# Threshold attention and feed-forward in one kernel: fewer weight chunks in the first six slots, diagonals given later, another end for the last tile

## The chip, the cores and the metric

The kernel runs on one core of a Trainium2 chip. The metric is device time in microseconds (us) from the start of the program to its end. The kernel before takes 1440.85 us, the median of three runs (1439.65 to 1445.99). The execution that was profiled took 1440.71 us and its profile spans 1438.9 us. Below, PE is TensorE, ACT ScalarE, DVE VectorE, POOL GpSimd and SP SyncE.

## What is computed

For 8 batches and 8 heads of 576 tokens and 64 features, attention keeps only scores close to the row's maximum; the heads are then laid side by side (512 features), and a feed-forward block with a layer norm ahead of it is added to its own input:

```python
scores = scale * np.matmul(q, k.transpose(0, 1, 3, 2))
thresh = np.max(scores, axis=-1, keepdims=True) - tau
scores = np.where(scores >= thresh, scores, -1000000000.0)
scores = scores - np.max(scores, axis=-1, keepdims=True)
attn = np.exp(scores)
attn = attn / (np.sum(attn, axis=-1, keepdims=True) + 1e-09)
x = np.matmul(attn, v)                      # then (B, H, S, D) -> (B, S, H*D)
...
mu = np.mean(x, axis=-1, keepdims=True)
var = np.mean((x - mu) ** 2, axis=-1, keepdims=True)
xn = (x - mu) / np.sqrt(var + 1e-06) * g_ln
ch = np.maximum(xn @ w_ch1, 0.0) @ w_ch2    # 512 -> 2048 -> 512
out = x + ch
```

The weights come as 64-bit floats, so the kernel has to turn them into 32-bit floats itself.

## The kernel before

**Slots.** Each batch is done in `SLOTS` = 9 slots, 72 in all (the loop at L750). A slot takes 512 rows of scores: of one pair of heads, or, in the middle slot of a batch (`s == HP` = 4), what is left of all four pairs. A slot's attention work is: scores on PE (L384) into two PSUM areas; row maxima on DVE (L398) and thresholds on POOL (L402); exponentials on ACT (L409); mask and sum on DVE (L416) and a reciprocal (L420). Then the weights are turned and multiplied with the values (L538) in the next slot.

**Two ways of turning.** In batch 0 (slots 0 to 8) `turn_weights` multiplies them on PE with a diagonal matrix that holds the reciprocals (`tp` L100, `tr` L468). The four diagonals are made on ACT (L427), and the products are copied from PSUM by ACT (`em` L462, `rest` L477). From slot 9 on, `turn_blocks` scales on POOL (L429), transposes on DVE (`et`, L494), stores to DRAM (`scr`, L500) and loads back (L509, L510).

**Feed-forward.** The 4608 tokens form 16 groups of 288, two to a batch. When group g has all its attention output, PE makes its mean (L573), DVE subtracts it (`xc`, L579), and `ffn_steps` is put into a queue. It has 16 steps of the first product (`p1`, each ended by a relu on ACT, L649), the variance with its inverse root on DVE (`root`, L616), and four output tiles `p2` of 16 steps each. `add_to_x` multiplies an output tile on DVE (L596) and adds x on POOL (L597); `store` transposes it on DVE (L602); `send` stores it by four DMAs on SP (L609). `second_part` (L703) deals out these PE steps over the four quarters of each slot, at a rate set by `ready(g)` (L696): the quarter in which group g comes in. Group 0 is ready at quarter 24 (slot 6), group 1 at 42 (slot 10).

**Buffers.** PE's products outside the scores share the PSUM tag `ff`, which has two buffers: `tp`, `tr`, `p1`, `p2`, `mean`, `var`, and `pv` in the first slots.

**Weight conversion.** `Weights` cuts both matrices into 32 chunks of 128 by 512 numbers, 16 of each matrix. `fetch` loads a chunk by a DMA on SP (L243), `begin` starts it with two operations on DVE (L263, L267) and two on ACT (L271, L275), `carry` adds on POOL (L281), `mask` is one DVE operation (L290), and `end` scales chunks of the first matrix on ACT (L303). One `tick` does the next such part of up to four chunks, in the order end, mask, carry, begin. A slot has up to six ticks; the first six slots use `ticks` (L752): two in slots 0 to 2 and three in slots 3 to 5. So 15 chunks are begun when slot 6 starts. Raw and half-made chunks lie in borrowed memory (`w2`, `hidden`, `et`, `x`, and `stage`); a number beside each piece says up to which chunk it may be used (L210 to L216). A feed-forward step is held back until its chunks are given.

**Order.** Every engine carries out its instructions in the order in which this code gives them; nothing is reordered by a planner. `aside`, `stores` and `at_quarter` are lists of calls that are given later, at fixed points of the loop.

Of the kernel before, what the change touches and what calls it, by code (L numbers as in the profile page):

```python
# [8 lines left out]
F32 = mybir.dt.float32  # L9
# [3 lines left out]
ALU = mybir.AluOpType  # L13
# [5 lines left out]
def kernel(  # L19
# [31 lines left out]
    nc = tc.nc  # L51
# [4 lines left out]
    HP = H // 2  # L56
    NK = DM // 128
# [3 lines left out]
    TOK = S // 2  # L61
    QH = 256
    SLOTS = 2 * HP + 1
    NG = 2 * B
# [9 lines left out]
    ffn = ctx.enter_context(tc.tile_pool(name="ffn", bufs=2))  # L74
# [8 lines left out]
    ident = consts.tile([128, 128], F32, name="ident")  # L83
# [6 lines left out]
    hidden = consts.tile([128, ND, TOK], F32, name="hidden")  # L90
# [33 lines left out]
    def load_v(u):  # L124
# [13 lines left out]
        out=tau_sb, in_=bass.AP(tensor=tau.tensor, offset=tau.offset, ap=[[0, 128], [1, 1]])  # L138
# [5 lines left out]
    for t in rests + v_rest:  # L144
# [9 lines left out]
        out=scl_sb, in0=tau_sb, scalar1=0.0, scalar2=SCALE, op0=ALU.is_ge, op1=ALU.mult  # L154
# [11 lines left out]
    class Weights:  # L166
# [13 lines left out]
        def __init__(self):  # L180
            self.chunks = [
                (w1_sb[i][:, c : c + WC], w_ch1[i * 128 : (i + 1) * 128, c : c + WC], i)
                for c in range(0, DF, WC)
                for i in range(NK)
            ] + [
                (
                    w2_sb[:, m, d : d + 4].rearrange("p d c -> p (d c)"),
                    w_ch2[d * 128 : (d + 4) * 128, m * 128 : (m + 1) * 128].rearrange(
                        "(d p) c -> p d c", p=128
                    ),  # L190
                    None,
                )
                for m in range(NK)
                for d in range(0, ND, 4)
            ]
            self.n1 = NK * (DF // WC)
            self.fetched = self.begun = self.carried = self.masked = self.ended = 0
            self.raw, self.made, self.due, self.ticks = {}, {}, [], 2
            flat = lambda t: t.rearrange("p a b -> p (a b)")

            x_room = ffn.tile([128, NK, TOK], F32, tag="x", bufs=3, name="x_room")
            stage = consts.tile([128, 8, WC], F32, name="stage")
            et = att.tile([128, NB, 128], F32, tag="et", bufs=1, name="et0")

            n1 = self.n1
            self.free = []
            for t, n, before in (  # L210
                (w2_sb.rearrange("p m d c -> p (m d) c"), ND // 2, lambda p: n1 + 2 * p),
                (hidden, 4, lambda p: 10),
                (et, 2, lambda p: 2 * n1),
                (x_room, 1, lambda p: 2 * n1),
                (stage, 4, lambda p: 2 * n1),
            ):  # L216
                for p in range(n):
                    self.free.append((before(p), -1, flat(t)[:, p * 2 * WC : (p + 1) * 2 * WC]))
# [87 lines left out]
        def tick(self):  # L306
            self.ticks += 1
            if self.ended < self.masked:
                self.end()
            if self.masked < self.carried and self.due[self.masked] <= self.ticks:  # L310
                self.mask()
            if self.carried < self.begun:
                self.carry()
            if self.begun < self.fetched:
                self.begin()
# [95 lines left out]
    def weights(es, thr, divide):  # L411


        den = small.tile([128, 4], F32, tag="den", name="den")
        for i in range(4):
            nc.vector.scalar_tensor_tensor(  # L416
                out=es[:, i], in0=blocks[i], scalar=thr[:, i : i + 1], in1=es[:, i],
                op0=ALU.is_ge, op1=ALU.mult, accum_out=den[:, i : i + 1],
            )
        nc.vector.reciprocal(den, den)  # L420
        diags = []
        for i in range(4):
            if not divide:
                if i % 2 == 0:
                    two = ffn.tile([128, TOK], F32, tag="o", bufs=6, name="diag")
                diags.append(two[:, i % 2 * 128 : i % 2 * 128 + 128])
                nc.scalar.mul(diags[i], ident, den[:, i : i + 1])  # L427
                continue
            nc.gpsimd.tensor_scalar(  # L429
                out=es[:, i], in0=es[:, i], scalar1=den[:, i : i + 1], scalar2=1.0,  # L430
                op0=ALU.mult, op1=ALU.mult,
            )
        return diags


# [77 lines left out]
    groups, sums = {}, {}  # L513
# [74 lines left out]
    def run_all(calls):  # L588
        now = calls[:]
        calls.clear()  # L590
        for fn in now:
            fn()

    def add_to_x(g, m, p2, rb):
        o = ffn.tile([128, TOK], F32, tag="o", bufs=6, name="o")
        nc.vector.tensor_mul(o, p2, rb)  # L596
        nc.gpsimd.tensor_tensor(out=o, in0=o, in1=groups[g][:, m], op=ALU.add)  # L597
        aside.append(lambda: store(g, m, o))

    def store(g, m, o):  # L600
# [4 lines left out]
    def send(g, m, ot):  # L605
        b, t = divmod(g, 2)
        for i in range(4):
            f = m * 128 + 32 * i
            nc.sync.dma_start(  # L609
                out=out[b, t * TOK : (t + 1) * TOK, f : f + 32].rearrange(  # L610
                    "(n r) c -> r n c", r=32
                ),
                in_=ot[32 * i : 32 * i + 32].rearrange("p (n c) -> p n c", c=32),
            )
# [81 lines left out]
    def ready(g):  # L696

        if g < 2:
            return (24, 42)[g]
        b, t = divmod(g, 2)  # L700
        return QUARTERS * (b * SLOTS + (HP, 2 * HP)[t] + 2) + (2, 4)[t]

    def second_part(n, i):  # L703

        nonlocal issued, owed
        if not queue:
            return
        at = QUARTERS * n + i
        g = issued // STEPS
        left = sum(ROOM[t % QUARTERS] for t in range(at, ready(g + 1))) if g + 1 < NG else 0  # L710
        owed += ((g + 1) * STEPS - issued) * ROOM[i] / left if left > 0 else 8


        got = 1 if i in (0, QUARTERS - 1) else 2
        while queue and (owed >= 0.5 or got == 1 and i in (0, QUARTERS - 1)):
            got = next(queue[0], None)
            if got is None:
                queue.pop(0)
                got = 1
            elif got == 0:  # L720
                owed = 0.0
                break
            else:
                issued += 1
                owed -= 1
# [7 lines left out]
    conversion = Weights()  # L733
# [15 lines left out]
    load_v(1)  # L749
    for n in range(NS):  # L750
        b, s = divmod(n, SLOTS)
        ticks = (1, 3, 4)[: 2 + n // 3] if n < 6 else range(1, 7)  # L752

        def tick(i):
            if i in ticks:
                conversion.tick()

        scores(b, s)
        run(n, -1)
        rest = exponentials()  # L760
        es, thr = next(rest)
        run(n, 0)
        conversion.fetch(2)
        run_all(stores)
        second_part(n, 0)
        next(rest, None)

        u = (n + 1) // SLOTS * HP + (n + 1) % SLOTS
        if (n + 1) % SLOTS < HP and u < len(units):
            turn(u)  # L770
            if u + 1 < len(units):
                load_qk(u + 1)
        run_all(aside)
        tick(1)
        run(n, 1)
        second_part(n, 1)
        tick(2)
        blocks_go = by_blocks(b * HP)
        diags = weights(es, thr, blocks_go)
        run_all(aside)  # L780
        run_all(stores)
        tick(3)
        run(n, 2)
        second_part(n, 2)
        tick(4)
        box = []
        if blocks_go:
            scr = turn_blocks(s, es)
            at_quarter(n + 1, 0, lambda s=s, scr=scr, box=box: box.append(fetch(s, scr)))
        else:  # L790
            made = turn_weights(s, es, diags)
            at_quarter(n + 1, -1, next, made)
            at_quarter(
                n + 1, 0 if s <= HP else -1, lambda made=made, box=box: box.append(next(made))
            )
        at_quarter(
            n + 1, 1 if b == 0 and s <= HP else 3,
            lambda b=b, s=s, box=box: values_of(b, s, box[0]),
        )
        if s in (HP, 2 * HP):  # L800
            group_ready(2 * b + (s > HP))
        run_all(aside)
        conversion.fetch(2)
        tick(5)
        run(n, 3)
        if b == 0 and s < HP - 2:
            load_v(s + 2)
        elif n >= SLOTS - 2 and (n + 2) % SLOTS < HP and n < NS - 2:
            load_v((n + 2) // SLOTS * HP + (n + 2) % SLOTS)
        second_part(n, 3)  # L810
        tick(6)
        run_all(aside)
# [37 lines left out]
```

## Time and profile before

| stretch, us | length | PE busy | DVE busy | ACT busy | what it is |
|---|---|---|---|---|---|
| 14.00 to 50.63 | 36.63 | 26.90 | 32.03 | 25.46 | slots 0 to 2 |
| 50.63 to 93.11 | 42.48 | 31.24 | 42.07 | 35.92 | slots 3 to 5 |
| 93.11 to 182.00 | 88.89 | 81.22 | 74.39 | 56.27 | slots 6 to 8, half of 9 |
| 182.00 to 1432.70 | 1250.70 | 1246.51 | 718.76 | 302.98 | the rest, to the last product |
| 1432.70 to 1438.90 | 6.20 | 0.00 | 0.94 | 0.00 | the end |

A stretch in which an engine is busy for nearly its whole length is set by that engine. A slot begins on DVE with two L398: at 50.63, 65.17, 79.68, 93.11, 123.20, 149.08, 168.44 and 194.94 for slots 3 to 10. In a timeline a line gives start, duration, engine, line of the kernel, operation, what is written from what, and count; in brackets how long the engine had been idle and what ended that. SPq is the queue of DMAs that SP gives.

### The profile page before, as it was taken

What the parts mean: (1) busy time and instruction counts of PE and PEld (TensorE: products, weight loads), DVE (VectorE), ACT (ScalarE), POOL (GpSimd) and SP (SyncE); (2) the same over time, 40 slices, a digit from 0 to 9 for tenths busy, and PEclk for the clock granted to TensorE, in tenths of its full rate; (3) what the DMA queues carried; (4) which work ended last, traced back from release to release, by engine and by line L of the source; (5) the groups of instructions that cost most, each with busy time, mean ns of one, the idle gap of its engine ahead of it and who ended that gap; (6) DMA issues with size and microseconds to landing.
All of it is one profiled execution on the core that took longest, in us unless ns stands there. A gap on an engine that the chain in (4) does not pass through costs nothing.

```text
span 1438.9 us, 29660 instructions
## 1 busy us (share of the span) xinstructions
PE 1389.7 (97%) x12168; PEld 852.3 (59%) x12168; DVE 870.5 (60%) x1492; ACT 421.9 (29%) x818; POOL 439.5 (31%) x681
## 2 busy tenths in 40 slices
PE   4879999999999999999999999999999999999998
PEld 3655665655556555655556555665556555565664
DVE  5998857556665666556665565656665666656111
ACT  3886513132222313132221312213132222213020
POOL 2344342333323233232322233232332323222100
PEclk8999999999999999999999999999999999999999
DMA  9622456558855587557855577556775578455301
GB/s 226 173 70 82 90 130 164 163 136 172 178 145 144 142 182 169 143 134 170 188 152 145 147 151 175 142 145 146 173 177 146 131 170 185 135 145 136 79 6 17
DMA packets 466840, 205.12 MB, mean 143 GB/s; under 512 B 275024, under 2 KB 428368, under 8 KB 466704
## 3 DMA queue, kind: packets, MB, share of 16 engines
q1 hardware_dynamic: 461936, 202.64, 57.9%
q8 instruction: 95, 1.56, 0.5%
q10 hardware_dynamic: 4736, 0.59, 0.4%
q14 instruction: 41, 0.34, 0.1%
q0 software_dynamic: 32, 0.00, 0.0%
HBM read 119.41 MB, written 83.76 MB: 141 GB/s over the span
## 4 chain that ended last, share of the span: by engine, by line
PE 89%; DVE 4%; ACT 2%; SPq 1%; issue 1%; DMA 1%; POOL 0%; POOLq 0%; ACTq 0%; DVEq 0%
PE p L100 67%; PE sc L538 10%; PE sc L384 10%; PE tp L100 1%; DVE e L416 1%; DMA em<-scr 1%; DVE neg L398 1%; SPq L500 1%; PE mean L100 0%; PE var L100 0%; DVE w L263 0%; ACT e L409 0%; PE tr L468 0%; SPq L129 0%; SPq L133 0%
## 5 line engine op out<-in xcount | busy, mean ns | idle before, releaser
L100 PE MATMUL p<-xc,w 128*64 128x288 f32 x4096 | 517.5, 408 | 6.5 <-ACT hidden L649 4.5
L100 PE MATMUL p<-hidden,w 128*64 128x288 f32 x4096 | 513.6, 407 | 0.0
L100 PEld LDWEIGHTS p<-xc,w 128*64 128x64 f32 x4096 | 291.8, 137 | 216.3 <-ACT hidden L649 14.4
L100 PEld LDWEIGHTS p<-hidden,w 128*64 128x64 f32 x4096 | 295.3, 137 | 199.1 <-issue 9.3
L398 DVE TENSOR_REDUCE neg<-sc 128x2 f32<-128x1152 f32 x144 | 188.8, 1352 | 250.1 <-PE sc L384 250.1
L409 ACT ACTIVATE e<-sc,neg 128x576 f32<-128x576 f32 x288 | 194.4, 742 | 261.7 <-DVE neg L398 256.2
L429 POOL TENSOR_SCALAR e<-e,den 128x576 f32<-128x576 f32 x252 | 188.5, 766 | 240.5 <-DVE den L420 240.4
L416 DVE SCALAR_TENSOR_TENSOR e<-sc,thr,e 128x576 f32<-128x576 f32 x288 | 219.1, 811 | 27.8 <-ACT e L409 27.8
L494 DVE STREAM_TRANSPOSE et<-e 128x1152 f32<-128x1152 f32 x112 | 153.6, 1375 | 78.3 <-POOL e L429 58.2
L649 ACT ACTIVATE hidden<-p 128x288 f32<-128x288 f32 x256 | 105.7, 413 | 284.5 <-PE p L100 282.9
L384 PE MATMUL sc<-kT,qT 64*128 64x384 f32 (+3 forms) x1024 | 150.2, 424 | 20.0 <-DVE qT L344 10.1
L402 POOL TENSOR_SCALAR thr<-neg,low_sb 128x2 f32<-128x2 f32 x144 | 41.9, 291 | 352.2 <-DVE neg L398 343.3
L384 PEld LDWEIGHTS sc<-kT,qT 64*128 64x128 f32 x1024 | 94.2, 191 | 77.2 <-issue 27.5
L538 PE MATMUL sc<-em,v_in 128*64 128x256 f32 (+1 forms) x1408 | 131.4, 330 | 2.1 <-DMA em<-scr 2.1
L555 ACT COPY x<-sc 128x256 f32<-128x256 f32 x60 | 22.3, 372 | 316.9 <-PE sc L538 291.9
L538 PEld LDWEIGHTS sc<-em,v_in 128*64 128x64 f32 x1408 | 86.2, 138 | 41.6 <-issue 2.9
L597 POOL TENSOR_TENSOR o<-o,x 128x288 f32<-128x288 f32 x64 | 51.4, 804 | 151.4 <-DVE o L596 151.4
L596 DVE TENSOR_TENSOR o<-p,rb 128x288 f32<-128x288 f32 x64 | 28.1, 439 | 103.5 <-PE p L100 103.0
L564 POOL TENSOR_TENSOR sum<-sum,x 128x256 f32<-128x256 f32 (+1 forms) x64 | 32.7, 511 | 71.8 <-ACT x L555 69.3
L655 POOL TENSOR_TENSOR sq<-sq 128x288 f32<-128x288 f32 x48 | 38.8, 808 | 42.1 <-ACT sq L653 39.6
L564 POOL TENSOR_TENSOR sum<-x 128x256 f32<-128x256 f32 (+1 forms) x32 | 16.7, 523 | 98.8 <-ACT x L555 57.3
L538 PE MATMUL sc<-rest,v_rest 128*64 128x256 f32 (+1 forms) x352 | 44.4, 329 | 0.0
(130 smaller groups left out, 715.0 us busy)
## 6 DMA issues: line engine op xcount, KB each, us to landing
scr<-et SPq DMA_DIRECT2D x252, 288.0 KB, 4.8
em<-scr SPq DMA_DIRECT2D x63, 1024.0 KB, 5.9
out_dram<-ot SPq DMA_DIRECT2D x256, 36.0 KB, 4.2
q_in<-in_q_dram SPq DMA_DIRECT2D x124, 72.0 KB, 3.4
k_in<-in_k_dram SPq DMA_DIRECT2D x120, 72.0 KB, 2.6
v_in<-in_v_dram SPq DMA_DIRECT2D x64, 128.0 KB, 4.5
rest<-scr SPq DMA_DIRECT2D x63, 128.0 KB, 5.9
w<-in_moe_w_ch_dram SPq DMA_DIRECT2D x10, 512.0 KB, 5.9
```

Source lines behind the costliest of these rows:

```text
L100: nc.tensor.matmul(out[r], lhsT=lhsT[:, r], rhs=rhs, **flags)
L384: nc.tensor.matmul(sc[h][64 * i : 64 * i + 64 if s == HP else 128, at : at + n], lhsT=ql[r] if s == HP else qT[r, half, j * 128 : (j + 1) ...
L398: nc.vector.tensor_reduce(out=neg[:, i], in_=pairs[h], axis=AXL.X, op=ALU.max, negate=True,)
L402: nc.gpsimd.tensor_scalar(out=thr[:, i], in0=neg[:, i], scalar1=-1.0, scalar2=low_sb, op0=ALU.mult, op1=ALU.add,)
L409: nc.scalar.activation(es[:, i], blocks[i], func=AF.Exp, bias=neg[:, i : i + 1])
L416: nc.vector.scalar_tensor_tensor(out=es[:, i], in0=blocks[i], scalar=thr[:, i : i + 1], in1=es[:, i], op0=ALU.is_ge, op1=ALU.mult, accum_o ...
L429: nc.gpsimd.tensor_scalar(out=es[:, i], in0=es[:, i], scalar1=den[:, i : i + 1], scalar2=1.0, op0=ALU.mult, op1=ALU.mult,)
L494: nc.vector.transpose(et[:, :, 64 * h : 64 * h + 64].rearrange("p n (j c) -> p j n c", j=2), es[:, 2 * h : 2 * h + 2].rearrange("p j (n c) ...
L538: nc.tensor.matmul(dst[64 * h : 64 * h + 64], lhsT=vt[:, c, h, :] if c < J else vr[:, h, :], rhs=pick(em[:, c] if c < J else er, hp, h), s ...
L564: nc.gpsimd.tensor_tensor(out=sums[g][:, cols], in0=x[:, 0, cols] if c == 1 else sums[g][:, cols], in1=x[:, c, cols], op=ALU.add,)
L597: nc.gpsimd.tensor_tensor(out=o, in0=o, in1=groups[g][:, m], op=ALU.add)
L649: nc.scalar.activation(hidden[:, d], p1, func=AF.Relu)
```

## The change

Five edits go together.

1. `ticks` is `(1, 3)` in all of the first six slots. So 12 chunks instead of 15 are begun when slot 6 starts, and the rest follow from slot 6 on. The borrowed pieces of `hidden` may be used only up to chunk 7 (before: 9), because the feed-forward writes `hidden` from slot 6 on; those of `et` only up to chunk 27 (before: 31). In slots 5 to 8 there is one more `fetch`.
2. The diagonals are taken out of `weights` into `diagonals`. In slots 0 to 4 and 8 they are given where they were; in slots 5 to 7 only after the third tick and the feed-forward steps of quarter 2. The aim is that relus on ACT don't stand behind diagonals that wait for DVE.
3. Group 1 is ready at quarter 43 instead of 42.
4. The last output tile of all (`g == NG - 1`, `m == NK - 1`) is added to x on DVE instead of POOL.
5. Its four stores are given by two queues, SP and ACT in turn, instead of SP alone.

```diff
-                (hidden, 4, lambda p: 10),
-                (et, 2, lambda p: 2 * n1),
+                (hidden, 4, lambda p: 8),
+                (et, 2, lambda p: 28),
...
-        diags = []
-        for i in range(4):
-            if not divide:
-                if i % 2 == 0:
-                    two = ffn.tile([128, TOK], F32, tag="o", bufs=6, name="diag")
-                diags.append(two[:, i % 2 * 128 : i % 2 * 128 + 128])
-                nc.scalar.mul(diags[i], ident, den[:, i : i + 1])
-                continue
+        for i in range(4 if divide else 0):
...
+        return den
+
+    def diagonals(den):
+
+        diags = []
+        for i in range(4):
+            if i % 2 == 0:
+                two = ffn.tile([128, TOK], F32, tag="o", bufs=6, name="diag")
+            diags.append(two[:, i % 2 * 128 : i % 2 * 128 + 128])
+            nc.scalar.mul(diags[i], ident, den[:, i : i + 1])
         return diags
...
-        nc.gpsimd.tensor_tensor(out=o, in0=o, in1=groups[g][:, m], op=ALU.add)
+        last = (g, m) == (NG - 1, NK - 1)
+        engine = nc.vector if last else nc.gpsimd
+        engine.tensor_tensor(out=o, in0=o, in1=groups[g][:, m], op=ALU.add)
...
-            nc.sync.dma_start(
+            last = (g, m) == (NG - 1, NK - 1)
+            (nc.scalar if last and i % 2 else nc.sync).dma_start(
...
-            return (24, 42)[g]
+            return (24, 43)[g]
...
-        ticks = (1, 3, 4)[: 2 + n // 3] if n < 6 else range(1, 7)
+        ticks = (1, 3) if n < 6 else range(1, 7)
...
-        diags = weights(es, thr, blocks_go)
+        den = weights(es, thr, blocks_go)
+        if n <= HP or n == 2 * HP:
+            diags = diagonals(den)
         run_all(aside)
         run_all(stores)
+        if HP < n < SLOTS:
+            conversion.fetch(2)
         tick(3)
         run(n, 2)
         second_part(n, 2)
+        if HP < n < 2 * HP:
+            diags = diagonals(den)
         tick(4)
```

## The prediction

> **What bounds the kernel now.** First the page's busy shares and 40 slices, then five stretches of the span by engine.
>
> ```profile
> PE 1389.7 (97%) x12168; PEld 852.3 (59%) x12168; DVE 870.5 (60%) x1492; ACT 421.9 (29%) x818; POOL 439.5 (31%) x681
> ...
> 50.63:93.11 42.48, 31.24 (x404) 23.99 (x400) 42.07 (x66) 35.92 (x72) 20.10 (x23) 1.00 0.35 106
> 93.11:182.00 88.89, 81.22 (x773) 54.65 (x775) 74.39 (x118) 56.27 (x108) 36.48 (x36) 0.98 0.32 82
> 182.00:1432.70 1250.70, 1246.51 (x10731) 751.04 (x10727) 718.76 (x1241) 302.98 (x589) 366.76 (x594) 1.00 0.60 145
> 1432.70:1438.90 6.20, 0.00 (x0) 0.00 (x0) 0.94 (x2) 0.00 (x0) 0.79 (x1) 0.83 0.15 24
> ```
>
> Columns: stretch, length, busy time of PE, PEld, DVE, ACT, POOL, clock, DMA share, GB/s. From 182 us to the last matmul PE idles 4 of 1251 us, so its work there is fixed and the time is that work plus the idle time ahead of and behind it. Only two places can give anything: the first 182 us and the last 6.2. Slots 3 to 5 (50.63 to 93.11, between the pairs of row maxima, L398) are VectorE's: busy 42.07 of 42.48 us. Its timeline at the end of slot 3:
>
> ```profile
> 59.00 0.18 DVE L420 RECIPROCAL den<-den 128x4 f32<-128x4 f32 x1
> 59.10 1.22 DVE L290 SCALAR_TENSOR_TENSOR hidden<-hidden 128x512 f32<-128x512 f32 x1
> 60.24 1.52 DVE L263 TENSOR_SCALAR w<-w 128x512 uint32<-128x512 uint32 x1
> 61.80 0.69 DVE L267 SCALAR_TENSOR_TENSOR w<-w 128x512 uint32<-128x512 uint32 x1
> 62.41 0.69 DVE L290 SCALAR_TENSOR_TENSOR hidden<-hidden 128x512 f32<-128x512 f32 x1
> 63.01 1.52 DVE L263 TENSOR_SCALAR w<-w 128x512 uint32<-128x512 uint32 x1
> 64.56 0.69 DVE L267 SCALAR_TENSOR_TENSOR w<-w 128x512 uint32<-128x512 uint32 x1
> 65.17 2.61 DVE L398 TENSOR_REDUCE neg<-sc 128x2 f32<-128x1152 f32 x2
> ```
>
> Two ticks of weight conversion (mask L290, begin L263 and L267) stand between the reciprocal and the next maxima. In slots 6 to 9 PE's gaps end with ScalarE:
>
> ```profile
> 93.61 2.87 PE L100 MATMUL tp<-diag,e 128*64 128x128 f32 x48 [1.81 <-ACT em L462]
> 106.16 2.16 PE L100 MATMUL p<-xc,w 128*64 128x288 f32 x16 [1.00 <-ACT hidden L649]
> 111.08 3.81 PE L100 MATMUL p<-xc,w 128*64 128x288 f32 x20 [2.76 <-ACT hidden L649]
> 170.05 1.09 PE L100 MATMUL tp<-diag,e 128*64 128x128 f32 x16 [0.69 <-ACT em L462]
> ```
>
> **What the Trainium skill says.** "SBUF — State Buffer", Who interferes with whom: a VectorE instruction with two SBUF inputs, or a tensor_scalar in two-port mode, blocks against GpSimd, for the whole instruction. The trace agrees: L263 takes 0.42 us at 53.76 but 1.52 at 63.01, beside GpSimd's carry (L281, 62.66 to 64.24). "PSUM — Partial Sum Buffer", Engine vs sequencer instructions: ScalarE's, VectorE's and GpSimd's queues are strict FIFO. It agrees: the relu at 110.63 comes behind two ticks and four diagonals although its product was ready. "Perfetto Trace Analysis", Optimization Strategy: a repeating gap on the saturated engine can mean too few buffers for the next tile. The gap before the second, third and fourth `tp` of slot 9 (0.69, 0.68, 0.68 us) is that: an open `p2` leaves one of two `ff` buffers. "DMA: Bandwidth & Descriptors", Issuing engines are not separate DMA queues: a second issuing engine saves only issue time.
>
> **The change part by part.**
>
> Third tick out of slots 3 to 5. In slots 3 and 4 it is 62.41 to 65.17 and 76.92 to 79.68: 2.76 us each. PE's scores of the next slot end at 61.2, before 62.41, so VectorE stays the limit. ScalarE then has per slot exponentials 2.6, copies 2.1 + 0.5 + 0.3, diagonals 1.2 and two ticks of 1.75 (its three lines L303, L271, L275 together): 10.2 us, in a slot that falls from 14.5 to 11.8. Gain 5.5 us. In slot 5 PE sets the next step: scores end 90.22, mean 90.76. There ScalarE's fourth-tick work disappears and the diagonals go behind the third tick's three ops; they end about 90.9, so the copies of `em` no longer hold PE 1.81 us. First product of the feed-forward about 1.9 us earlier. Together 7.4.
>
> Diagonals later in slots 6 and 7. In slot 6 the relus go ahead of the diagonals. With exponentials ending 1.9 us earlier I place the relu of step 2 at 103.85 in the old count, so the next product waits 0.8 instead of 1.0; then two ticks (3.5 us) still stand ahead of the relu of step 3, so 1.85 instead of 2.76. Gain 1.1. In slot 7 the first tick now carries a scaling (L303, 0.61) ahead of a relu: loss 0.6.
>
> Twelve chunks instead of 15 are begun when slot 6 starts. Slots 6 and 7 begin six each as before; the surplus lands in slot 8 (five begun instead of four) and slot 9 (three instead of one). In slot 8 PE's step is 21.5 us against VectorE's 12.2 up to the sums L416, so PE doesn't wait there.
>
> Group 1 ready one quarter later, with late chunks 30 and 31. This is where I expect the gain to go. In the order in which the changed code gives instructions, `mean` of group 1 comes in slot 10 after 16 matmuls of the third output tile and 12 of the fourth. Both tiles hold an `ff` buffer, so `mean` waits for VectorE to read the third (L596), which is queued behind slot 10's maxima, transposes, a mask and four L416. In the kernel before, that tile ended in slot 9 and was read at 191.78, ahead of `mean` at 197.24. Ahead of those maxima VectorE also has the begins of chunks 30 and 31, whose loads find no free piece before the second fetch of slot 9 and so are queued on SyncE behind the four `scr` stores, which wait for the transposes of `et`. Behind those begins on VectorE stand all of slot 10's sums, and PE waits for them through that one buffer. Lines for the prices:
>
> ```profile
> 184.27 2.84 DVE L494 STREAM_TRANSPOSE et<-e 128x1152 f32<-128x1152 f32 x2 [0.57 <-POOL e L429]
> 187.13 3.80 SPq L500 DMA_DIRECT2D scr<-et  x4
> 159.59 0.44 SPq L243 DMA_DIRECT2D et<-in_moe_w_ch_dram  x1
> 165.52 0.69 ACT L271 ACTIVATE et<-et 128x512 int32<-128x512 uint32 x1 [0.20 <-DMA et<-in_moe_w_ch_dram]
> ```
>
> Count from S, the start of slot 9's scores on PE (166.13 before). L416 ended S+15.3 before, set by ScalarE's copies; VectorE comes later now, 15.5 taken. To the end of the transposes 5.5 (181.5 to 187.0): S+21. `scr` issue 3.9, two loads and landing 5.9 (159.59 to 165.5): S+31. Begin and carry block 1.6, `ot` 0.5, maxima 2.6, transposes with their wait 2.2, mask 0.7, L416 and reciprocal 3.1, L596 0.4: about S+42. PE needs scores 2.1, `tp`, `tr` and gaps 8.0, 52 matmuls at 0.243 = 12.6, values 2.2: slot 10 begins S+24.9, then 2.1 + 28 x 0.243: it wants `mean` at S+33.9. New wait about 8.2 us. Bounds: if the loads land ahead of VectorE's need, only L416's queue counts, some 2.3; if VectorE enters slot 9 5 us late and the loads take longer, 11. I take 8.2. A single 0.7 us wait of PE at 204.2 (on L596) falls away.
>
> Tail. The last tile: multiply 1432.73, GpSimd 1433.34 to 1434.13, transpose 1434.16; an add on VectorE (0.45, as L596) starts the transpose at about 1433.7: 0.45. Four stores took SyncE 1.81 us to issue; two each on two queues save 0.9. ScalarE is idle there. Gain 1.35.
>
> Pieces of `hidden` only to chunk 7 and `et` only to chunk 27, and the extra fetch in slots 5 to 8: loads change places, none is added; in slots 0 to 5 they land ahead of use as before. Zero.
>
> Sum: 7.4 + 1.1 - 0.6 - 8.2 + 0.7 + 1.35 = 1.75; 1440.85 - 1.75 = 1439.1.
>
> **Rivals.** (a) The wait in slot 10 is short, 2.3 us: for it speaks that loads of 512 KB landed in 4.7 us too, and that the tick order may fall better; against it, FIFO order. Gain 7.65: 1433.2, and near 1432 if slot 6 loses its gaps altogether. (b) No gain early: ScalarE takes VectorE's place in slots 3 to 5 (35.92 of 42.48 us busy already), saving only 3 us instead of 7.4, with the same wait in slot 10. Sum -2.65: 1443.5, slower. Against it: the two-tick slot 1 took 11.7 us with 2.2 of transposes besides. (c) VectorE, still loaded in slots 7 and 8 (25.9 us of work in slot 7, all busy), is so late that slot 9's scores wait too and the slot 10 wait reaches 11: another 3 to 6 us, 1442 to 1445.
>
> **How the numbers follow.** Forecast 0.60, (a) 0.24, (b) 0.06, (c) 0.10. Predicted time 1439.1. The range takes in the forecast with both ends of the slot 10 wait (1433.2 to 1442) and the near half of (c): 1432.5 to 1443. Half a per cent is 7.2 us: under 1433.6 only most of (a), 0.20; over 1448 only the far edge of (c), 0.03; between them 0.77.
>
> **What would show it.** Right: maxima of slots 3, 4 and 5 about 11.8 us apart; first feed-forward product near 89.8; a PE gap of some 8 us before `mean` L100 in slot 10, released by L596's successor; VectorE idle in slot 9 for a weight load; last store issued 1.35 us sooner after the last matmul. Wrong: that gap under 3 us (then 1433), slots 3 to 5 still over 13 us, or new PE gaps before L384 in slots 7 to 9.

## The result and the profile after

The changed kernel takes 1450.35 us (median of 6 runs, 1449.02 to 1456.76), the kernel before in the same session 1440.96 us: ratio 1.0067, 95% interval 1.0045 to 1.009. It is 9.4 us slower. The forecast was 1439.1, at most 1443. The profiled span grew from 1438.9 to 1448.2 us.

PE first: the timeline of the changed kernel, its pieces with a gap ahead of them, and the first product of the feed-forward. (Its line numbers run up to 6 higher than before: L416 and earlier are unchanged, the copy of the values is L558, the relu L655, the multiply of an output tile L599, the `scr` stores L503.)

```profile
87.29 2.87 PE L100 MATMUL tp<-diag,e 128*64 128x128 f32 x48 [0.74 <-ACT em L465]
...
90.86 7.97 PE L100 MATMUL p<-xc,w 128*64 128x288 f32 x64
...
99.83 2.16 PE L100 MATMUL p<-xc,w 128*64 128x288 f32 x16 [1.00 <-ACT hidden L655]
103.58 1.68 PE L100 MATMUL p<-xc,w 128*64 128x288 f32 x12 [1.59 <-ACT hidden L655]
122.34 6.53 PE L100 MATMUL p<-xc,w 128*64 128x288 f32 x52 [1.35 <-ACT hidden L655]
156.74 3.73 PE L384 MATMUL sc<-kT,qT 64*128 64x384 f32 x16 [2.52 <-ACT x L558]
...
193.26 4.21 PE L384 MATMUL sc<-kT,qT 64*128 64x384 f32 x16 [9.77 <-ACT x L558]
206.75 0.71 PE L100 MATMUL mean<-sum,avg_sb 128*64 128x288 f32 x4 [1.95 <-DVE o L599]
```

Down to 104 us it goes much as forecast: the `em` wait is 0.74 instead of 1.81, the first product starts at 90.86 instead of 97.18, the gap of 2.76 is 1.59. Then three new waits stand where the kernel before had none: the scores of slot 9 (2.52), the scores of slot 10 (9.77) and `mean` (1.95). The first two end with ScalarE's copy of the values. In the stretches (columns as before: length, then busy PE, PEld, DVE, ACT, POOL, clock, DMA share, GB/s) the gain and the loss stand side by side:

```profile
50.00:85.00 35.00, 25.52 (x325) 20.01 (x322) 34.69 (x46) 28.76 (x56) 15.35 (x16) 1.00 0.39 115
85.00:200.00 115.00, 105.58 (x1018) 72.98 (x1016) 92.29 (x151) 67.08 (x130) 48.63 (x52) 0.99 0.34 89
...
50.00:85.00 35.00, 30.37 (x402) 23.82 (x400) 34.39 (x52) 31.20 (x62) 14.67 (x19) 1.00 0.29 84
85.00:200.00 115.00, 95.14 (x875) 66.04 (x876) 89.13 (x135) 63.23 (x123) 46.42 (x46) 0.94 0.39 102
```

The first two lines are the kernel before, the other two the changed one. PE is busy 4.85 us more in the first stretch and 10.4 us less between 85 and 200, at a lower clock. The cause is read across the engines, from the timeline around 190 us:

```profile
181.33 4.20 SPq L503 DMA_DIRECT2D scr<-et  x4
...
181.85 0.68 PE L541 MATMUL sc<-rest,v_rest 128*64 128x256 f32 x4
...
182.28 1.21 PE L100 MATMUL p<-hidden,w 128*64 128x288 f32 x8
185.63 2.86 SPq L243 DMA_DIRECT2D stage<-in_moe_w_ch_dram  x2
...
191.70 0.68 ACT L271 ACTIVATE stage<-stage 128x512 int32<-128x512 uint32 x1 [18.66 <-DMA stage<-in_moe_w_ch_dram]
191.70 0.43 DVE L263 TENSOR_SCALAR x_room<-stage 128x512 uint32<-128x512 uint32 x1 [10.05 <-DMA stage<-in_moe_w_ch_dram]
...
192.27 0.68 ACT L275 ACTIVATE x_room<-stage 128x512 f32<-128x512 f32 x1
192.83 0.38 ACT L558 COPY x<-sc 128x256 f32<-128x256 f32 x1
193.26 4.21 PE L384 MATMUL sc<-kT,qT 64*128 64x384 f32 x16 [9.77 <-ACT x L558]
```

The values' product L541 is finished at 182.5. Its copy L558 could run then, but on ScalarE it stands behind the begin of chunk 30 (L271), which has waited 18.66 us for its load. That load was issued at 185.63, behind the four `scr` stores, and landed about 6 us later. PE's next scores write the PSUM area `sc` of which the values fill the last 256 columns, and they wait for the copy.

The tail gave what it should:

```profile
1443.19 0.46 DVE L599 TENSOR_TENSOR o<-p,rb 128x288 f32<-128x288 f32 x1 [5.92 <-PE p L100]
1443.68 0.46 DVE L602 TENSOR_TENSOR o<-o,x 128x288 f32<-128x288 f32 x1
1444.18 0.48 DVE L607 STREAM_TRANSPOSE ot<-o 128x288 f32<-128x288 f32 x1
1444.69 0.89 ACTq L615 DMA_DIRECT2D out_dram<-ot  x2
```

From the multiply to the end of the span it is 5.0 us, 6.2 before. The two stores on ACT's queue take 0.89 us to issue, where four on one queue took 1.81: that is the issue time which the prediction expected to save.

### The profile page after: what moved, and what is told of

Its sections match the earlier page's. It is cut to its first block, busy times and chain, and to the rows that moved or that the text cites. A ratio compares the mean times of both kernels' runs of the same rounds, so it can differ in the third digit from the quotient of the medians.

```text
span 1448.2 us, 29660 instructions
## 1 busy us (share of the span) xinstructions
PE 1392.3 (96%) x12168; PEld 855.2 (59%) x12168; DVE 871.8 (60%) x1493; ACT 421.3 (29%) x818; POOL 437.7 (30%) x680
## 4 chain that ended last, share of the span: by engine, by line
PE 87%; DVE 7%; ACT 2%; issue 1%; DMA 1%; POOL 1%; SPq 0%; POOLq 0%; ACTq 0%; DVEq 0%
PE p L100 64%; PE sc L384 10%; PE sc L541 10%; DVE e L416 2%; DVE neg L398 1%; PE tp L100 1%; ACT e L409 1%; DVE w L290 1%; PE mean L100 1%; DVE w L263 0%; DMA em<-scr 0%; DMA stage<-in_moe_w_ch_dram 0%; POOL e L422 0%; PE var L100 0%; ACT em L465 0%
## 5 line engine op out<-in xcount | busy, mean ns | idle before, releaser
L416 DVE SCALAR_TENSOR_TENSOR e<-sc,thr,e 128x576 f32<-128x576 f32 x288 | 219.3, 812 | 20.5 <-ACT e L409 20.5
L655 ACT ACTIVATE hidden<-p 128x288 f32<-128x288 f32 x256 | 105.5, 412 | 275.7 <-PE p L100 274.0
L384 PE MATMUL sc<-kT,qT 64*128 64x384 f32 (+3 forms) x1024 | 154.0, 433 | 32.5 <-ACT x L558 12.4
L384 PEld LDWEIGHTS sc<-kT,qT 64*128 64x128 f32 x1024 | 96.2, 194 | 91.0 <-issue 27.8
L541 PE MATMUL sc<-em,v_in 128*64 128x256 f32 (+1 forms) x1408 | 130.8, 329 | 0.6 <-DMA em<-scr 0.4
L558 ACT COPY x<-sc 128x256 f32<-128x256 f32 x60 | 22.3, 372 | 316.9 <-PE sc L541 293.7
L541 PEld LDWEIGHTS sc<-em,v_in 128*64 128x64 f32 x1408 | 86.1, 137 | 39.3 <-DVE et L497 1.5
L599 DVE TENSOR_TENSOR o<-p,rb 128x288 f32<-128x288 f32 x64 | 28.1, 439 | 106.4 <-PE p L100 105.8
L567 POOL TENSOR_TENSOR sum<-x 128x256 f32<-128x256 f32 (+1 forms) x32 | 16.8, 525 | 102.8 <-ACT x L558 59.1
L541 PE MATMUL sc<-rest,v_rest 128*64 128x256 f32 (+1 forms) x352 | 44.3, 329 | 0.0
```

The costliest lines, as they stand in the source:

```text
L384: nc.tensor.matmul(sc[h][64 * i : 64 * i + 64 if s == HP else 128, at : at + n], lhsT=ql[r] if s == HP else qT[r, half, j * 128 : (j + 1) ...
L416: nc.vector.scalar_tensor_tensor(out=es[:, i], in0=blocks[i], scalar=thr[:, i : i + 1], in1=es[:, i], op0=ALU.is_ge, op1=ALU.mult, accum_o ...
L541: nc.tensor.matmul(dst[64 * h : 64 * h + 64], lhsT=vt[:, c, h, :] if c < J else vr[:, h, :], rhs=pick(em[:, c] if c < J else er, hp, h), s ...
L567: nc.gpsimd.tensor_tensor(out=sums[g][:, cols], in0=x[:, 0, cols] if c == 1 else sums[g][:, cols], in1=x[:, c, cols], op=ALU.add,)
L655: nc.scalar.activation(hidden[:, d], p1, func=AF.Relu)
```

## The experiments

The kernel before was run again beside each group of experiments: 1441.68 us (59 runs) for the tail, the diagonals, the copy given earlier and the load given earlier; 1441.75 (34) for the ticks alone and the three other runs with early loads or quarter 42 in the changed kernel; 1441.53 (48) for the other four. A ratio is to that kernel, with its 95% interval.

### The edits alone

**Edits 4 and 5, the tail.**

```diff
-        nc.gpsimd.tensor_tensor(out=o, in0=o, in1=groups[g][:, m], op=ALU.add)
+        engine = nc.vector if last else nc.gpsimd
+        engine.tensor_tensor(out=o, in0=o, in1=groups[g][:, m], op=ALU.add)
...
+            (nc.scalar if last and i % 2 else nc.sync).dma_start(
```

> The kernel before with only edits 4 and 5 (last tile added on VectorE, its stores by two queues). All theories: 1.1 to 1.4 us faster than before (ratio 0.9990 to 0.9993): the transpose of the last tile starts 0.45 us sooner and the last store is issued 0.9 us sooner. Nothing before 1432 us moves.

Measured 1440.57 us, ratio 0.9992 (0.9984 to 0.9999): about 1.1 us faster.

**Edit 2, the diagonals.**

```diff
+        den = weights(es, thr, blocks_go)
+        if n <= HP or n == 2 * HP:
+            diags = diagonals(den)
...
+        if HP < n < 2 * HP:
+            diags = diagonals(den)
```

> The kernel before with only edit 2 (diagonals of slots 5 to 7 given later), three ticks kept in slots 3 to 5. If the diagonals ahead of the relus are what holds PE in slot 6: the wait of 2.76 us there falls by about 1.2 us and the time by 1 to 2 us. If the two weight ticks ahead of the relu are: no change over 0.7 us.

Measured 1439.85 us, ratio 0.9986 (0.9976 to 0.9997): about 1.8 us faster. In its profile the `em` wait in slot 6 is 1.35 instead of 1.81, the second gap of slot 6 is 1.60 instead of 2.76, and the gap of slot 7 stays at 0.63:

```profile
93.88 2.87 PE L100 MATMUL tp<-diag,e 128*64 128x128 f32 x48 [1.35 <-ACT em L465]
...
110.18 2.65 PE L100 MATMUL p<-xc,w 128*64 128x288 f32 x20 [1.60 <-ACT hidden L652]
```

Part of the gain in this profile is PE's clock. Behind the gap of 2.76 us the same 20 matmuls took 3.81 us before (the line at 111.08 in the prediction), because the clock was halved from 112.4 to 115.8 (0.50 in the stretch 113 to 114); behind the gap of 1.60 they take 2.65. The loss in slot 7 that I had put down to this edit is edit 1's: with the ticks alone (next run) that gap is 1.22 us.

**Edit 1, the ticks** (with the pieces given up earlier and the extra fetch that belong to it).

```diff
-                (hidden, 4, lambda p: 10),
-                (et, 2, lambda p: 2 * n1),
+                (hidden, 4, lambda p: 8),
+                (et, 2, lambda p: 28),
...
-        ticks = (1, 3, 4)[: 2 + n // 3] if n < 6 else range(1, 7)
+        ticks = (1, 3) if n < 6 else range(1, 7)
...
+        if HP < n < SLOTS:
+            conversion.fetch(2)
```

> The kernel before with edit 1 alone (ticks 1 and 3, the pieces of hidden and et given up earlier, the extra fetch), diagonals, quarter and tail as before. Theory A (edit 1 carries the whole loss): scores of slot 10 wait 9 us or more behind a copy of the values that stands behind a late chunk on ScalarE; without the 2 us of the diagonals and 1.2 us of the tail the time is 1449 to 1453 us. Rival B (the loss needs edits 1 and 3 together): the wait stays under 4 us, 1438 to 1441 us.

Measured 1453.04 us, ratio 1.0075 (1.0063 to 1.0088). From its PE timeline:

```profile
193.48 3.70 PE L384 MATMUL sc<-kT,qT 64*128 64x384 f32 x16 [6.26 <-ACT x L555]
204.38 6.96 PE L100 MATMUL p<-hidden,w 128*64 128x288 f32 x32 [3.65 <-DVE w L290]
```

The time is at the upper end of theory A's: edit 1 alone loses 11.3 us. The wait for the copy is smaller than expected, 6.26 instead of 9, and a second one of 3.65 us comes up that I hadn't named: a product waits for the mask of its weights (L290), the last step of a chunk's conversion. Both come from chunks that are converted late, but not both from the late loads: with early loads and quarter 42 (below) the wait for the mask is 3.65 us all the same.

### What holds PE: the copy, or the load behind which it stands?

**The copy given earlier.** In slots 8 and 9 the values' product and its copy come ahead of the fifth tick, so the copy no longer stands behind that tick's begins.

```diff
-        tick(5)
+        if n not in (SLOTS - 1, SLOTS):
+            tick(5)
         run(n, 3)
+        if n in (SLOTS - 1, SLOTS):
+            tick(5)
```

> The changed kernel with the copy L558 of the values given ahead of the fifth tick in slots 8 and 9 (only the order on ScalarE changes). Theory A, the copy behind the late chunk on ScalarE is the whole loss: PE's wait of 9.8 us ahead of slot 10's scores goes and nothing takes its place; time about 1438 to 1440. Theory B, VectorE's queue would have made PE wait anyway: the scores start at about 184, but VectorE still gets its late weights at 191.7 and reads the third output tile near 206, so PE waits 10 to 12 us ahead of mean instead; time 1447 to 1450.

Measured 1450.65 us, ratio 1.0056 (1.0038 to 1.0075): no gain over the changed kernel, and so theory B, with both the time and the wait a little above what it named. Its timeline shows where the gain went:

```profile
180.37 0.37 ACT L558 COPY x<-sc 128x256 f32<-128x256 f32 x1 [9.52 <-PE sc L541]
181.22 2.21 PE L384 MATMUL sc<-kT,qT 64*128 64x384 f32 x16
...
189.97 0.43 DVE L263 TENSOR_SCALAR x_room<-stage 128x512 uint32<-128x512 uint32 x1 [10.55 <-DMA stage<-in_moe_w_ch_dram]
...
202.52 0.43 DVE L599 TENSOR_TENSOR o<-p,rb 128x288 f32<-128x288 f32 x1
...
203.09 1.23 PE L100 MATMUL mean<-sum,avg_sb 128*64 128x288 f32 x4 [12.72 <-DVE o L599]
```

The copy runs as soon as its product is done and the scores of slot 10 start without a wait (slot 9's still wait 1.44 us). So the scores do wait for the copy, and the copy's place on ScalarE was what made it late. But VectorE stands before the same load until 189.97, so it reads the third output tile (L599) only at 202.52, and `mean` waits 12.72 us for that buffer. This is the wait that the prediction described, at 12.7 instead of 8.2 us. In the changed kernel it is hidden behind the earlier one.

**The load given earlier.** The two last loads are put on SP ahead of slot 9's `scr` stores, and nothing else is changed.

```diff
+        if n == SLOTS:
+            conversion.fetch(2)
         if blocks_go:
             scr = turn_blocks
```

> The changed kernel with the second fetch of slot 9 moved ahead of the stores of the turned weights, so that the loads of chunks 30 and 31 are queued on SyncE ahead of them (order of loads only). Theory C, the late loads are the root of both waits: they land 6 to 8 us sooner, PE's wait ahead of slot 10's scores falls to 0 to 3 us; time 1440 to 1443. If the loads' place in the queue is not the cause: no change, 1449 to 1451.

Measured 1440.99 us, ratio 0.9995 (0.9984 to 1.0005): theory C, the 9.4 us are back.

```profile
176.16 0.95 SPq L243 DMA_DIRECT2D stage<-in_moe_w_ch_dram  x2
...
178.92 4.61 SPq L503 DMA_DIRECT2D scr<-et  x4
...
180.24 0.43 DVE L263 TENSOR_SCALAR x_room<-stage 128x512 uint32<-128x512 uint32 x1 [1.01 <-DMA stage<-in_moe_w_ch_dram]
181.41 0.37 ACT L558 COPY x<-sc 128x256 f32<-128x256 f32 x1
...
181.83 2.21 PE L384 MATMUL sc<-kT,qT 64*128 64x384 f32 x16 [0.73 <-ACT x L558]
...
193.32 1.23 PE L100 MATMUL mean<-sum,avg_sb 128*64 128x288 f32 x4 [2.34 <-DVE o L599]
```

The loads go out 9.5 us earlier and are there at 180.24 instead of 191.70, and with them VectorE's and ScalarE's begins and the copy come earlier. Of PE's waits in slot 10 0.73 us is left instead of 9.77, and `mean` waits 2.34, where the run with the copy alone had 12.72. With the two runs together the order of causes is settled: the loads behind the stores are the root, the copy is only the first way by which they reach PE.

### The quarter of group 1, and what is left with early loads

**Edit 3 undone**, `ready` of group 1 at 42 again.

```diff
-            return (24, 43)[g]
+            return (24, 42)[g]
```

> The changed kernel with group 1 ready at quarter 42 again (edit 3 undone). Theory A (the late loads of chunks 30 and 31 hold PE through ScalarE's copy of the values; the quarter is no part of it): the third output tile ends ahead of slot 10, so the mean of group 1 no longer waits (1.95 us before), but slot 10's scores still wait some 9 to 10 us for the copy L558: 1447 to 1450 us. Rival B (edit 3 is a root of the loss): the score wait falls under 3 us and the time to 1440 or 1441.

Measured 1448.39 us, ratio 1.0044 (1.0031 to 1.0056). `mean` no longer waits; the scores of slot 10 wait 6.03 us, and a product waits 3.65 us for a mask, as with the ticks alone. Theory A in the main, with the wait for the copy too high by 3 to 4 us. Edit 3 is no root of the loss. Whether it costs a little can't be said from this: the interval overlaps that of the changed kernel. Slot 9's scores wait 0.38 us here instead of 2.52. That goes with the quarter in every profile: with 43 they wait 1.39 to 2.54 us for the copy, with 42 and edit 1 at most 0.43.

**Early loads and 42.** (The two diffs above together.)

> The changed kernel with the two loads of chunks 30 and 31 given ahead of slot 9's scr stores, and group 1 ready at 42. Theory A (with early loads what is left of the loss is the mean that waits 2.34 us for the third output tile, and that is edit 3's): that wait vanishes, scores of slot 10 wait under 1.5 us, 1437.5 to 1439.5 us. Rival B (PE, earlier at the mean, meets DVE's backlog a step later, at the fourth output tile or the next slot's weights): 1440 to 1441.5 us, as with early loads alone.

Measured 1440.38 us, ratio 0.9993 (0.9986 to 1.0).

```profile
193.60 0.68 DVE L290 SCALAR_TENSOR_TENSOR w<-x_room 128x512 f32<-128x512 f32 x1
...
194.34 3.43 PE L100 MATMUL p<-hidden,w 128*64 128x288 f32 x16 [3.65 <-DVE w L290]
```

Rival B: the 2.34 us of `mean` are gone, and PE, earlier by that, waits 3.65 us for the mask of chunk 30, which stands on VectorE behind slot 10's maxima, transposes and subtractions of the mean.

**The same with the copy earlier.** (The copy's diff added.)

> As the run with early loads and quarter 42, and the copy of the values given ahead of the fifth tick in slots 8 and 9. Theory A (the copy stands behind begins of chunks on ScalarE in slot 9 too, and that alone holds the scores there): the wait of slot 9's scores falls from 2.52 to about 1.4 us, that of slot 10 to nothing; 0.5 to 1.5 us faster than without it, 1436.5 to 1438.5 us. Rival B (the ScalarE work that the copy passes turns up as a later wait, as the late loads did when the copy alone was moved): no difference from the run without it.

Measured 1440.85 us, ratio 0.9991 (0.9983 to 0.9999): no difference, rival B. With 42 the scores of slot 9 and 10 had only 0.4 us of waits left for the copy to save, and the waits for masks are 3.65 and 0.71.

**Early loads and `et` free up to chunk 29.**

```diff
-                (et, 2, lambda p: 28),
+                (et, 2, lambda p: 30),
+        if n == SLOTS:
+            conversion.fetch(2)
```

> The changed kernel with early loads, and the pieces of et free for chunks up to 29 instead of 27, so that six chunks are begun in slot 8 and two in slot 9. Theory A (the lateness of the last begins in slot 9 is what is left): the waits of slot 10 (0.73 and 2.34 us with early loads) shrink to 1.5 us together, slot 9's grows by less than 1 us: 1438.5 to 1440.5 us. Rival B (one more chunk ahead of slot 9's scores on ScalarE puts the copy of the values later still): slot 9's wait grows from 2.5 to 4 us or more, 1441 to 1443 us.

Measured 1441.12 us, ratio 0.9996 (0.9988 to 1.0004). The time lies in rival B's range, but the waits are neither's: slot 9's stays at 2.54, and those of slot 10 are 1.60 and 2.03, together 3.6, not 1.5. Six begins in slot 8 instead of five don't help: VectorE is busy for 17.4 of the 18 us from 139 to 157, which is slot 8.

In these four, whatever moves, one of the late chunks meets PE. What is left is the number of chunks that slots 8 to 10 have to convert: 12 are begun when slot 6 starts, slots 6 and 7 take 12 more, and 8 remain (5 in the kernel before).

### A version that keeps the gains

**Edits 2, 4 and 5 without 1 and 3.** (The diffs of the first two experiments together.)

> The kernel before with edits 2, 4 and 5 only. Theory A (the edits add up, since they lie in different places: 2.0 us for the diagonals, 1.2 us for the tail): 3.2 us faster than before, 1437.5 to 1438.5 us. Rival B (PE that is earlier by the diagonals' 2 us waits for a late weight chunk in slot 9 or 10): no faster than either alone, 1439.5 to 1441 us.

Measured 1438.24 us, ratio 0.9977 (0.9963 to 0.9991): 3.3 us faster, theory A. The two alone add up to 2.9, which is the same within the intervals.

**The third tick kept in slots 4 and 5**, with group 1 at 42 and all else as in the changed kernel.

```diff
-        ticks = (1, 3) if n < 6 else range(1, 7)
+        ticks = (1, 3) if n < 4 else (1, 3, 4) if n < 6 else range(1, 7)
...
-            return (24, 43)[g]
+            return (24, 42)[g]
```

> The changed kernel with the third tick kept in slots 4 and 5 (taken out of slot 3 alone, so that 14 chunks are begun when slot 6 starts and no mask is left for slot 10), group 1 ready at 42. Theory A (what is lost depends on how many chunks are left for slots 8 and 9: with one shifted instead of three the early gain of slot 3, 2.8 us, is kept): waits of PE in slots 9 and 10 as in the kernel before, under 1.5 us more; 2.8 us of slot 3, 2 us of the diagonals, 1.2 us of the tail: 1435 to 1437.5 us. Rival B (PE 2.8 us earlier meets the weights of slots 8 to 10 as late as ever, since VectorE's work up to there is the same): the gain of slot 3 is given back, 1437.5 to 1440 us.

Measured 1436.26 us (5 runs), ratio 0.9957 (0.9943 to 0.997): 5.3 us faster than the kernel before, and so some 15 us faster than the changed one (5.3 + 9.4). That is in theory A's range.

```profile
90.71 2.87 PE L100 MATMUL tp<-diag,e 128*64 128x128 f32 x48 [1.84 <-ACT em L465]
...
94.28 7.97 PE L100 MATMUL p<-xc,w 128*64 128x288 f32 x64
...
191.51 0.66 PE L100 MATMUL mean<-sum,avg_sb 128*64 128x288 f32 x4
...
199.20 3.13 PE L100 MATMUL p<-xc,w 128*64 128x288 f32 x24 [0.74 <-DVE o L599]
```

The first product starts 2.9 us earlier than before (94.28 against 97.18). No wait stands ahead of slot 9's or 10's scores. `mean` of group 1 comes at 191.51, 5.7 us earlier than before, and the one 0.74 us wait after it is the old one. SP issues all loads ahead of the first `scr` store. One chunk shifted out of the full slots costs nothing later, three cost all. This run keeps edit 1's earlier limits on `hidden` and `et`, so the limits alone don't make the last loads late.

**The same with 43.**

> As the run with the third tick kept in slots 4 and 5, but group 1 ready at 43 as in the changed kernel. Theory A (a mean at quarter 43 waits for the third output tile, about 2 us; and the later quarter spares a wait for a weight chunk of up to 3.7 us if there is one): within 1.5 us of the run with 42, on the slower side if that run shows no wait for a chunk. Rival B (with 43 the scores wait again for the copy of the values): 3 us or more slower than with 42.

Measured 1439.20 us, ratio 0.9979 (0.9972 to 0.9986). It is 2.9 us slower than with 42, between the two theories: the scores of slot 9 wait 1.39 us for the copy, `mean` 1.43 for L599, and later relus cost 3.5 us in five gaps (0.7 in one with 42). With 43 the products of group 0 are dealt out more thinly, so PE comes earlier to slot 9's scores, and the third output tile isn't over before slot 10.

## Why the prediction was wrong

**The early gain was right, a little large.** Forecast 7.4 us. The maxima of slots 3 to 5 lie 11.7 us apart (50.96, 62.70, 74.43), which is the 5.5 us of slots 3 and 4, and the first product is 6.3 us earlier. Slot 5 gave 1.1 instead of 1.9: of the `em` wait 0.74 us is left, where I had counted it gone. ScalarE isn't late there any more, since its copy at 86.66 waits 1.00 us for PE; the rest is the round of `tp` and copy through the `ff` buffers, as in the 0.69 us gaps of slot 9. Against that, 0.3 us were lost ahead of slot 3, in a stretch that the change doesn't touch.

**The diagonals were right in their waits.** Slot 6: 1.17 us gained (forecast 1.1, though split otherwise: gaps of 1.00 and 1.59 where 0.8 and 1.85 were forecast). Slot 7: 0.71 lost (forecast 0.6), through edit 1. Not forecast was that the shorter gap spares slot 6 the half clock.

**The step that failed** is the count of slot 10: "slot 10 begins S+24.9, then 2.1 + 28 x 0.243: it wants `mean` at S+33.9. New wait about 8.2 us." The root was right: loads of chunks 30 and 31 on SyncE behind the `scr` stores, landing 35 us after the start of slot 9's scores in the changed kernel (191.7 and 156.74); S+31 was forecast. But the count follows the late begin along VectorE alone, to `mean`. It lets PE start slot 10's scores without a wait. The same begin has two operations on ScalarE, and behind them in its queue stands the copy of the values. The count has no term for that copy, as if the scores did not need it: they write other columns, 128 to 1279, and the values 1280 to 1535. They do need it, and PE waits 9.77 us. In the same way "In slot 8 PE's step is 21.5 us against VectorE's 12.2 ... so PE doesn't wait there" weighs VectorE alone, and slot 9's scores waited 2.52 us for ScalarE.

What makes the scores need the copy? Both are in one PSUM area. The Trainium skill says in "PSUM — Partial Sum Buffer", PSUM bank collisions raise a hardware error, that PSUM is to be guarded by bank and quadrant and not by address; by the same page's Specifications (TRN2) a bank holds 512 FP32 values, so columns 1024 to 1535, with the values and the last of the scores, are one bank. The trace agrees that other columns are not enough: PE's scores start only when the copy ends (193.26 after 192.83 + 0.38, and with early loads 181.83 after 181.41 + 0.37). But it shows more than the page's rule asks. The matmul that waits is the first of the slot, which writes columns 128 to 511 (`64x384` in its line), in another bank than the copied ones. So the shared bank doesn't explain the wait as it stands. Whether it is set for the area as a whole, or only placed ahead of the first matmul, these runs don't tell.

The missing path is not the whole miss. With the copy given earlier, the path that was forecast stands alone, and it costs 12.72 us instead of 8.2; the kernel takes 1450.65 us, as long as with the copy late. There the loads have landed 33.8 us after the start of slot 9's scores instead of 31, and `mean`, wanted at 34.2 (forecast 33.9), starts at 46.9 instead of 42. So the wait for `mean` was mis-sized as well, by 4.5 us: transposes, loads and the queue behind them each took longer than counted.

**What that came to.** From the start of the first product to the end of the last one (the kernel before first) PE carries out the same matmuls:

```profile
97.18:1432.70 1335.52, 1324.17 (x11446) 802.25 (x11444) 789.12 (x1353) 357.05 (x693) 400.59 (x626) 1.00 0.58 141
...
90.86:1443.15 1352.29, 1326.64 (x11446) 804.97 (x11444) 797.53 (x1362) 361.24 (x702) 405.41 (x630) 0.99 0.58 141
```

The changed kernel takes 16.8 us more for them, where 7.0 was forecast (8.2 - 0.7 - 1.1 + 0.6). PE idles 14.3 us more: 9.77, 2.52 and 0.15 ahead of scores, 1.95 ahead of `mean`, 2.8 ahead of relus in the later slots (3.5 us in five gaps instead of 0.7 in one); less 0.5 in slots 6 and 7, 0.74 of the old wait on L596, and 1.5 ahead of the values' products in the later slots. The other 2.5 us are PE busy for longer with the same matmuls: the halved clock, which cost about 1.5 us in slot 9 and 2.3 in slot 10, less about 1.7 that it had cost before in slot 6. Three of these weren't in the forecast at all: the scores of slot 9, whose copy (156.35) stands on ScalarE behind four diagonals and three begins of slot 8; the clock; and the later relus, where I had taken PE's work from 182 us on as fixed.

**The rivals.** Rival (c) named the wait at slot 9's scores and gave 1442 to 1445, and gaps ahead of L384 were named as a sign of a wrong forecast. But (c) put them down to a late VectorE. They are ScalarE's, and the larger one is slot 10's. The sign "that gap under 3 us (then 1433)" misled: the gap ahead of `mean` is 1.95 us, but only because PE had lost 9.77 us just before.

**The tail was right**: 1.2 us of 1.35.

**Edit 3** was forecast as part of the loss, through the third output tile that ends after slot 10 has begun. That mechanism is there (1.95 in the changed kernel, 2.34 with early loads, 1.43 with the ticks kept), but it is small, and with late chunks the quarter 42 only exchanges it, and slot 9's wait, for the wait for a mask (3.65).

## What to carry to other kernels

When a load comes later, list everything that stands behind its first user on each engine's queue, and follow every such chain to the bound engine; here a cure for the nearest chain alone only uncovered the next. Treat instructions that use one PSUM area as dependent, whatever their columns, until a trace shows that they are not. Work that is taken out of a full stage has to fit into a later one before its deadline: here one chunk fitted and was worth keeping, three did not.

## What the runs showed of the hardware that was not expected

PE's clock fell in the long wait. Stretches of 1 us of the changed kernel:

```profile
187.00:188.00 1.00, 0.00 (x0) 0.00 (x0) 0.00 (x0) 0.00 (x0) 0.00 (x0) 1.00 0.76 177
188.00:189.00 1.00, 0.00 (x0) 0.00 (x0) 0.00 (x0) 0.00 (x0) 0.00 (x0) 0.50 0.88 168
...
197.00:198.00 1.00, 1.00 (x8) 0.35 (x6) 0.42 (x1) 0.00 (x0) 0.00 (x0) 0.50 0.48 94
198.00:199.00 1.00, 1.00 (x10) 0.60 (x8) 1.00 (x2) 0.03 (x1) 0.00 (x0) 0.88 0.45 73
199.00:200.00 1.00, 1.00 (x10) 0.56 (x8) 1.00 (x1) 1.00 (x2) 0.27 (x1) 1.00 0.18 28
```

PE stops at 183.5; the clock is halved from 188.0, 4.5 us later, and full again from about 198.2, 5.0 us after PE went on at 193.26. The 16 scores took 4.21 us instead of 2.21. The Trainium skill, "TensorE: Matmul & The Clock Gate", Part 1: The HAM clock gate, says that the clock is halved after an idle window of about 3.4 us and comes back after a busy one, and that the windows run free of the program. That agrees in kind for this wait.

But waits that are shorter than such a window halved it too:

```profile
93.43 4.51 PE L100 MATMUL tp<-diag,e 128*64 128x128 f32 x48 [1.98 <-ACT em L465]
```

This is the run with edits 2, 4 and 5: after a single wait of 1.98 us the clock was halved from 94.2 to 97.6, and the 48 matmuls took 4.51 us instead of 2.87. It does not happen each time. The same wait of 2.52 us ahead of slot 9's scores was followed by 3.73 us of scores in the changed kernel and by 2.21 in the run with early loads, which fits windows that run free. Each of these short waits was followed by some 3.4 us of half clock, or by none. So a wait of PE of 2 us or more is to be priced with up to 2 us on top, as an estimate from these cases.
